# Putting the main loop of a delta-rule attention and feed-forward kernel into program order, with the block inversion spread over three steps

## The chip, the cores and the metric

The kernel runs on one core of one Trainium2 chip. The metric is the device time of one execution in microseconds (us), the median of several executions. Every kernel was run beside the kernel before on the same chip; not every experiment was on one and the same chip, so ratios compare better across experiments than medians do.

Short names: PE is TensorE's matmul part and PEld its weight load, DVE is VectorE, ACT is ScalarE, POOL is GpSimd. L571 is line 571 of that kernel's file; line numbers differ between the kernels.

## The reference

```python
# attention: batch 4, 8 heads, 768 positions, 48 dims
for t in range(S):
    y[:, :, t] = einsum('bhd,bhde->bhe', q[:, :, t], state)
    v_old = einsum('bhde,bhd->bhe', state, k_n[:, :, t])        # k_n = k / (|k| + 1e-6)
    state = state + beta * einsum('bhd,bhe->bhde', k_n[:, :, t], v[:, :, t] - v_old)
# feed-forward on x = y as (3072 tokens, 384)
h = x @ w_in                                                    # 384 -> 2048
out = (maximum(h, 0) + alpha * minimum(h, 0)) @ w_out           # 2048 -> 384
```

All is float32. The kernel does the recurrence in chunks of 64 positions: 24 steps (12 chunks times two pairs of batches). In each step a 64x64 triangular system is solved for each head. Its inverse is put together from two 32x32 inverses, and those of four steps are eliminated together on VectorE ("the inversion"), so that one inversion serves four steps.

## The kernel before

The parts that matter, with cuts marked by `# ...`. A `weave` is a loop that takes from several generators in proportion, so that their instructions are written in a mixed order. Up to `opening.close()` the written order is kept; after it, the tool's scheduler orders the instructions of each engine anew.

```python
EARLY = 6                                    # key Grams and key flips run this many steps ahead

def flips(n_k, n_q):                         # transposes of keys and queries on PE
    # ...
    flip(early(n_k), p_k)
    nc.scalar.copy(k_t[n_k]..., p_k)         # key copy ahead of the query flip, same PSUM tile
    flip(q_pad[n_q % NQ], p_q)
    nc.scalar.copy(q_t[n_q]..., p_q)

def eliminate(m):                            # the inversion, on DVE
    r = block[m]
    nc.vector.tensor_tensor(out=r, in0=r, in1=inside, op=ALU.mult)
    # ...
    for j in range(1, HB - 1):               # 30 pairs of product and update
        nc.vector.tensor_tensor(out=prod, ...)
        nc.vector.tensor_tensor(out=r[...], ...)
        yield
    nc.vector.transpose(turned[m]..., r)     # two whole turns of 128x1024
    nc.vector.transpose(inverse[m]..., r...)
    yield

def ffn_in(c):                               # 48 matmuls, 8 groups of 6; a p_ffn tile each, bufs=2
    # ... six matmuls into p_h, then:
    nc.scalar.activation(low, p_h, ACT.Relu, scale=-1.0)
    for i in range(2):
        nc.vector.scalar_tensor_tensor(out=g[:, i], in0=low[:, i], ..., in1=p_h[:, i])

def attention(n):
    place(n + 1)                 # ACT writes diag (4 instructions), inv (2), wgt (2)
    through_state(n)             # PE; DVE r; ACT y
    yield
    solve(n)                     # PE; DVE u
    yield
    outputs(n)                   # PE, and the state's update; DVE y, state
    between_1(n + 1)             # PE; ACT mid
    grams(n + EARLY, n + 1)      # PE; DVE kk and masks; ACT and DVE gather the blocks
    yield
    between_2(n + 1); to_ffn(n); flips(n + EARLY + 1, n + 2); prep(n + EARLY + 1)
    # ... loads
    scale_v(n + 1)
    yield

opening.close()
for n in range(NJ, N):           # NJ = 4, N = 24
    gens = [(attention(n), 4)]
    if (n + 2) % NJ == 0 and n + 2 < N:
        gens.append((eliminate((n + 2) // NJ), HB))         # the whole inversion in one step
    # ... and half a chunk of the feed-forward: 40 of its 80 matmuls
    weave(*gens)
```

## Time and profile before

| | before |
|---|---|
| median of its first runs | 768.65 us |
| span of the profiled run | 767.8 us |
| opening, 0 to 181.5 us | PE busy 155.9 |
| steps 4 and 5, 181.5 to 214.5 | PE busy 31.9 |
| steps 6 to 23, 214.5 to 722.25 (507.75 us) | PE busy 492.6, DVE 241.5, ACT 143.7 |
| the last chunk, 722.25 to the end | PE busy 41.4 of 45.6 |

The busy times are from the windows of the trace. PE is nearly full, so only what leaves PE idle, or slows its clock, can be won. In the long loop that is 507.75 - 492.6 = 15 us of idleness, besides the time lost to a halved clock, which counts as busy.

### The profile page before, as it was taken

The page shows a single profiled execution, that of the slowest core. Times are in us where ns is not written, and L with a number is a line of the kernel's source. Part 1 is how long each engine was busy: PE and PEld are TensorE (multiplying, and loading weights), DVE is VectorE, ACT ScalarE, POOL GpSimd, SP SyncE. Part 2 cuts the span into 40 slices and gives each one's busy share as a digit, 9 for nine tenths or more (in the row PEclk, how much of TensorE's full clock was granted, in tenths as well). Part 3 has the DMA queues.
Part 4 walks back from the last instruction along what each step waited for, and adds up shares of the span by engine and source line. Part 5 has one row for each costly group of instructions (what it writes and reads, how often), then busy time and mean ns, then how long its engine had stood idle before and what let it go on. Part 6 is the DMA issues. An engine that isn't in the chain of part 4 may idle for free.

```text
span 767.8 us, 20517 instructions
## 1 busy us (share of the span) xinstructions
PE 721.8 (94%) x8987; PEld 517.9 (67%) x8987; DVE 412.2 (54%) x979; ACT 251.7 (33%) x563; POOL 21.5 (3%) x80
## 2 busy tenths in 40 slices
PE   5999888898998999998999998999999999999997
PEld 4546666555676678666678667678667677687774
DVE  5886788896599224596224596214596233132020
ACT  3416656514424234125134124123114223021110
POOL 5000000010000000000000000000000000000000
PEclk9999899999999999999999999999999999999999
DMA  6815564311321122121122121111111110100000
GB/s 120 215 39 144 136 175 99 81 25 32 64 47 31 30 43 43 23 42 34 31 43 44 22 43 22 33 32 32 22 33 33 22 35 10 22 12 2 21 0 21
DMA packets 110185, 37.61 MB, mean 49 GB/s; under 512 B 103392, under 2 KB 106480, under 8 KB 110096
## 3 DMA queue, kind: packets, MB, share of 16 engines
q1 hardware_dynamic: 110064, 36.29, 21.7%
q8 instruction: 71, 1.16, 0.6%
q14 instruction: 18, 0.15, 0.1%
q10 hardware_dynamic: 32, 0.01, 0.0%
HBM read 31.56 MB, written 4.72 MB: 47 GB/s over the span
## 4 chain that ended last, share of the span: by engine, by line
PE 57%; DVE 29%; ACT 6%; issue 6%; POOL 1%; DMA 1%; SPq 0%; POOLq 0%; DVEq 0%; ACTq 0%
PE p_ffn L601 24%; PE p_ffn L571 21%; DVE prod L413 7%; DVE block L419 7%; DVE g L582 2%; PE p_big L503 2%; PE p_big L353 2%; PE p_big L530 2%; PE p_big L517 1%; DVE block L399 1%; DVE turned L424 1%; ACT diag L439 1%; DVE inverse L426 1%; DVE kk L359 1%; PE p_big L536 1%
## 5 line engine op out<-in xcount | busy, mean ns | idle before, releaser
L571 PE MATMUL p_ffn<-xt,w_in 128*128 128x256 f32 x1152 | 275.1, 391 | 14.1 <-DVE g L582 6.9
L601 PE MATMUL p_ffn<-w_out,g 128*128 128x384 f32 x768 | 262.2, 494 | 3.8 <-ACT diag L439 2.9
L571 PEld LDWEIGHTS p_ffn<-xt,w_in 128*128 128x128 f32 x1152 | 215.6, 193 | 50.0 <-ACT space_out L202 5.5
L601 PEld LDWEIGHTS p_ffn<-w_out,g 128*128 128x128 f32 x768 | 143.5, 192 | 95.9 <-ACT diag L439 3.2
L582 DVE SCALAR_TENSOR_TENSOR g<-low,al_t,p_ffn 128x256 f32<-128x256 f32 x192 | 83.6, 477 | 127.2 <-ACT low L579 127.1
L579 ACT ACTIVATE low<-p_ffn 128x512 f32<-128x512 f32 x96 | 56.8, 593 | 96.5 <-PE p_ffn L571 88.5
L413 DVE TENSOR_TENSOR prod<-block 128x30 f32<-128x30 f32 (+9 forms) x180 | 59.3, 330 | 5.5
L419 DVE TENSOR_TENSOR block<-block,prod 128x30 f32<-128x30 f32 (+9 forms) x180 | 59.4, 330 | 5.1
L544 DVE TENSOR_TENSOR y<-y,p_big 128x384 f32<-128x384 f32 x22 | 12.1, 552 | 58.8 <-PE p_big L530 58.8
L607 ACT COPY o_sb<-p_ffn 128x384 f32<-128x384 f32 x24 | 11.5, 478 | 90.1 <-PE p_ffn L601 90.1
L663 PE MATMUL p_ffn<-k_t,ident 128*128 128x512 f32 x76 | 37.9, 647 | 0.0
L439 ACT ACTIVATE diag<-inverse,which 64x128 f32<-64x128 f32 (+1 forms) x72 | 28.7, 399 | 23.1 <-PE p_big L476 17.5
L467 ACT COPY mid<-p_big 128x256 f32<-128x256 f32 x24 | 8.8, 372 | 80.1 <-PE p_big L463 80.1
L506 DVE TENSOR_TENSOR r<-v_raw,p_big 128x384 f32<-128x384 f32 x22 | 12.0, 550 | 37.0 <-PE p_big L503 36.8
L481 DVE TENSOR_TENSOR inv<-inv,p_big 128x256 f32<-128x256 f32 x24 | 10.0, 417 | 37.2 <-PE p_big L476 36.5
L439 ACT ACTIVATE inv<-inverse,which 128x256 f32<-128x256 f32 x48 | 21.7, 500 | 24.7 <-PE p_big L517 24.5
L663 PEld LDWEIGHTS p_ffn<-k_t,ident 128*128 128x128 f32 x76 | 14.8, 204 | 16.2 <-issue 15.7
L439 ACT ACTIVATE diag<-turned,which 128x256 f32<-128x256 f32 x24 | 11.6, 506 | 39.5 <-DVE turned L424 39.4
L353 PE MATMUL p_big<-k_t 48*64 48x64 f32 x768 | 18.3, 239 | 6.2 <-ACT k_t L337 4.3
L476 PEld LDWEIGHTS p_big<-diag,mid 64*64 64x64 f32 x768 | 14.3, 141 | 13.7 <-issue 9.8
L306 DVE TENSOR_REDUCE norm<-ksq 128x8 f32<-128x384 f32 x24 | 13.1, 546 | 17.1 <-ACT ksq L304 17.1
L392 ACT ACTIVATE same<-kk,which 128x256 f32<-128x256 f32 x24 | 12.2, 508 | 29.5 <-DVE kk L359 29.4
(94 smaller groups left out, 634.6 us busy)
## 6 DMA issues: line engine op xcount, KB each, us to landing
w_out<-in_moe_w_in_dram SPq DMA_DIRECT2D x12, 512.0 KB, 5.5
qp<-in_q_dram SPq DMA_DIRECT2D x48, 96.0 KB, 2.9
v_raw<-in_v_dram SPq DMA_DIRECT2D x48, 96.0 KB, 2.8
kl<-in_k_dram SPq DMA_DIRECT2D x96, 48.0 KB, 2.7
out_dram<-o_sb SPq DMA_DIRECT2D x48, 96.0 KB, 2.2
ke<-in_k_dram SPq DMA_DIRECT2D x46, 96.0 KB, 3.0
space_out<-in_moe_w_out_dram SPq DMA_DIRECT2D x11, 384.0 KB, 3.7
w_out<-in_moe_w_out_dram SPq DMA_DIRECT2D x5, 384.0 KB, 3.7
```

Of the source, the lines that this page charges most:

```text
L353: nc.tensor.matmul(p[half(t ^ a if w else t), a, w, g], k_t[n][dims(a), g, half(t)], rhs[n][dims(a), g, half(t)],)
L413: nc.vector.tensor_tensor(out=prod, in0=r[:, 0:j, j : j + 1].to_broadcast([128, j, n]), in1=r[:, j : j + 1, j + 1 : HB].to_broadcast([128, ...
L419: nc.vector.tensor_tensor(out=r[:, 0:j, j + 1 : HB], in0=r[:, 0:j, j + 1 : HB], in1=prod, op=ALU.add)
L439: nc.scalar.mul(dst[n % NE][to or rows, a.start * G : a.stop * G, cols], src[m][rows, heads], which[rows, i : i + 1],)
L476: nc.tensor.matmul(p[half(t), a, g], mid[n % 2][half(t ^ a), a * G + g], diag[n % NE][half(t ^ a), a * G + g, HB:C],)
L503: nc.tensor.matmul(p[half(t), a, w, g], x[n][dims(a), g, half(t)], state[bp][dims(a), t, g])
L530: nc.tensor.matmul(p[half(t), a, g], a_t[n][half(t ^ a), a * G + g], us[n][half(t ^ a), a, g])
L571: nc.tensor.matmul(p_h[:, i], w_in[:, t, (f + i) * 128 : (f + i + 1) * 128], xt[:, t], start=(t == 0), stop=(t == KT - 1),)
L579: nc.scalar.activation(low, p_h, ACT.Relu, scale=-1.0)
L582: nc.vector.scalar_tensor_tensor(out=g[:, i], in0=low[:, i], scalar=al_t[:, f + i : f + i + 1], in1=p_h[:, i], op0=ALU.mult, op1=ALU.add,)
L601: nc.tensor.matmul(p_o[bp], gs[f // 2][:, f % 2, bp * 128 : (bp + 1) * 128], w_out[:, f], start=(f == 0), stop=(f == FT - 1),)
L663: nc.tensor.matmul(p, ident, k_t[NJ - 1].rearrange("p g i -> p (g i)"))
```

## The change

Its intent: keep the program's order everywhere, give each step four pieces that each leave a quarter of a step between a producer and its user, take the inversion over three steps rather than one, and so keep PE full. The key Grams run 8 steps ahead, which the longer inversion needs.

```diff
-EARLY = 6
+EARLY = 8
+FIRST = 6
-    opening.enter_context(tc.manual_schedule(engines={      # ended by opening.close() before the loop
+    ctx.enter_context(tc.manual_schedule(engines={          # never ended

     def flips(n_k, n_q):
-            nc.scalar.copy(k_t[n_k].rearrange("p g i -> p (g i)"), p_k)
+            copies.append((k_t[n_k], p_k))
         # ...
+        for dst, src in copies:
+            nc.scalar.copy(dst.rearrange("p g i -> p (g i)"), src)

+    PIECES = 4
+    def turns(dst, src):                                    # a block turn in four quarters
+        n = HB // PIECES
+        for i in range(PIECES):
+            nc.vector.transpose(dst(slice(n * i, n * i + n)), src(slice(n * i, n * i + n)))
+            yield

     def attention(n):
-        place(n + 1)
+        place(n + 1, (0,))
         through_state(n)
+        between_1(n + 1)
+        place(n + 1, (1, 2))
         yield
         solve(n)
+        grams(n + EARLY, N)
+        between_2(n + 1)
+        scale_v(n + 1)
         yield
         outputs(n)
-        between_1(n + 1)
-        grams(n + EARLY, n + 1)
-        yield
-        between_2(n + 1)
+        next_state(n)
+        grams(N, n + 1)
+        load_late(n + 2)
+        squares(n + EARLY + 1)                              # apart from their roots (weigh)
+        yield
+        flips(n + EARLY + 1, n + 2)
         to_ffn(n)
-        flips(n + EARLY + 1, n + 2)
-        prep(n + EARLY + 1)
+        weigh(n + EARLY + 1)
         # ...

     for n in range(NJ, N):
-        if (n + 2) % NJ == 0 and n + 2 < N:
-            gens.append((eliminate((n + 2) // NJ), HB))
+        if n % NJ == 0 and n < N - NJ:
+            m = n // NJ + 1
+            blocks, left = eliminate(m), WHOLE + (PIECES if m > 2 else 0)
+            share = -(-left // 3)
+        if n % NJ < 3 and n < N - NJ:
+            gens.append((part(blocks, share), share))
```

Cut here: the Gram's left half is written straight into the gathered block and the right half into a tile of its own; the first five steps need three ACT writes fewer each; twelve units of the second inversion move forward in the opening (`SOON = 12`); the Grams of steps 10 and 11 are caught up before the loop, beside a quarter of a feed-forward output.

More of the change, by code (lines that the diff above doesn't have):

```diff
@@ L138, in load_late @@
                     nc.sync.dma_start(out=dst[a][half(t ^ a), :, 0:D], in_=src[a])
-    opening = ExitStack()
-    opening.enter_context(tc.manual_schedule(engines={
+    ctx.enter_context(tc.manual_schedule(engines={
         mybir.EngineType.PE, mybir.EngineType.DVE, mybir.EngineType.Activation,
@@ L290 @@
         nc.gpsimd.memset(t, 0.0)
-    stats, k_t, q_t, kk, a_t = {}, {}, {}, {}, {}
+    right = [const.tile([128, H + 1, HB], FP32, name=f"right{i}") for i in range(EARLY)]
+    for t in right:
+        nc.gpsimd.memset(t[:, 0], 0.0)
+    stats, k_t, q_t, a_t = {}, {}, {}, {}
     def by_parity(x):
@@ L301, in prep, with squares @@
             return
-        c, bp = steps[n]
+        squares(n)
+        weigh(n)
+    def squares(n):
+        if n >= N:
+            return
         ksq = work.tile([128, H, D], FP32, name="ksq", bufs=1)
@@ L306, in prep, with weigh @@
         nc.vector.tensor_reduce(out=norm, in_=ksq, axis=AXX, op=ALU.add)
+        stats[n] = norm
+    def weigh(n):
+        if n >= N:
+            return
+        c, bp = steps[n]
+        norm = stats[n]
         nc.scalar.sqrt(norm, norm)
@@ L332, in flips @@
         p = ps_big() if both else None
+        copies = []
         if n_k < N:
@@ L341, in flips @@
             q_t[n_q] = work.tile([128, G, 128], FP32, name="q_t")
-            nc.scalar.copy(q_t[n_q].rearrange("p g i -> p (g i)"), p_q)
+            copies.append((q_t[n_q], p_q))
+        for dst, src in copies:
+            nc.scalar.copy(dst.rearrange("p g i -> p (g i)"), src)
     def quarters():
@@ L357, in grams @@
         if n_k < N:
-            kk[n_k] = work.tile([128, H, C], FP32, name="kk", bufs=EARLY)
-            nc.vector.tensor_tensor(
-                out=kk[n_k].rearrange("p (a g) i -> p a g i", a=2),
-                in0=p[:, :, 0],
-                in1=stats[n_k][1][:, 0:2, :, None].to_broadcast([128, 2, G, C]),
-                op=ALU.mult,
-            )
+            w = stats[n_k][1][:, 0:2, :, None].to_broadcast([128, 2, G, HB])
+            for dst, cols in (
+                (gather(n_k), slice(0, HB)), (right[n_k % EARLY][:, 1:], slice(HB, C))
+            ):
+                nc.vector.tensor_tensor(
+                    out=dst.rearrange("p (a g) i -> p a g i", a=2), in0=p[:, :, 0, :, cols],
+                    in1=w, op=ALU.mult,
+                )
             keep(n_k)
@@ L385, with gather @@
     same, block, inverse, turned = {}, {}, {}, {}
-    def keep(n):
+    def gather(n):
         m, j = n // NJ, n % NJ
@@ L391, in keep, with turn_in @@
             same[m] = work.tile([128, NJ, H, HB], FP32, name="same", bufs=1)
-        nc.scalar.mul(same[m][:, j], kk[n][:, :, 0:HB], which[:, 0:1])
-        nc.vector.scalar_tensor_tensor(
-            out=same[m][:, j], in0=kk[n][:, :, HB:C], scalar=which[:, 1:2], in1=same[m][:, j],
-            op0=ALU.mult, op1=ALU.add,
-        )
-        if j == NJ - 1:
-            block[m] = work.tile([128, HB, HB], FP32, name="block", bufs=1)
-            nc.vector.transpose(
-                block[m].rearrange("b r c -> b c r"), same[m].rearrange("r j h c -> r c (j h)")
-            )
+        return same[m][:, j]
+    def keep(n):
+        m, j = n // NJ, n % NJ
+        for t in range(2):
+            own = slice(64 * t + HB, 64 * t + C)
+            if n < NJ:
+                nc.vector.tensor_copy(out=same[m][own, j], in_=right[n % EARLY][own, 1:])
+            else:
+                nc.scalar.copy(same[m][own, j], right[n % EARLY][own, 1:])
+        if j == NJ - 1 and m <= 2:
+            for _ in turn_in(m):
+                pass
+    PIECES = 4
[4 more added lines that the diff above has]
+            yield
+    def turn_in(m):
+        block[m] = work.tile([128, HB, HB], FP32, name="block", bufs=1)
+        yield from turns(
+            lambda x: block[m][:, :, x].rearrange("b r c -> b c r"),
+            lambda x: same[m][:, :, :, x].rearrange("r j h c -> r c (j h)"),
+        )
     def eliminate(m):
+        if m > 2:
+            yield from turn_in(m)
         r = block[m]
@@ L423, in eliminate, with changes @@
         turned[m] = work.tile([128, NJ * H, HB], FP32, name="turned", bufs=1)
-        nc.vector.transpose(turned[m].rearrange("c b r -> c r b"), r)
+        yield from turns(
+            lambda x: turned[m][:, :, x].rearrange("c b r -> c r b"), lambda x: r[:, x]
+        )
         inverse[m] = work.tile([128, NJ * H, HB], FP32, name="inverse", bufs=1)
-        nc.vector.transpose(inverse[m].rearrange("r b c -> r c b"), r.rearrange("b r c -> b c r"))
-        yield
+        yield from turns(
+            lambda x: inverse[m][:, :, x].rearrange("r b c -> r c b"),
+            lambda x: r[:, :, x].rearrange("b r c -> b c r"),
+        )
+    WHOLE = HB - 1 + 2 * PIECES
+    def changes(n):
+        return n > NJ
     def place(n, parts=(0, 1, 2)):
@@ L446, in place @@
         if 1 in parts:
-            put(diag, second, inverse, 1, a=slice(0, 1))
-            for t in range(2):
-                put(diag, second, inverse, 1, half(t), half(1 - t), slice(1, 2))
+            put(diag, second, inverse, 1, a=slice(0, 1 if changes(n) else 2))
+            if changes(n):
+                for t in range(2):
+                    put(diag, second, inverse, 1, half(t), half(1 - t), slice(1, 2))
         if 2 in parts:
             put(inv, first, inverse, 0)
-            put(inv, second, inverse, 1)
+            if changes(n):
+                put(inv, second, inverse, 1)
             w = stats[n][1]
@@ L463, in between_1 @@
             nc.tensor.matmul(
-                p[half(t ^ a), a, g], kk[n][half(t), a * G + g],
+                p[half(t ^ a if changes(n) else t), a, g],
+                right[n % EARLY][half(t), a * G + g : a * G + g + 2].rearrange("p b i -> p (b i)"),
                 diag[n % NE][half(t), a * G + g, 0:HB],
@@ L475, in between_2 @@
         for g, a, t in quarters():
+            x = half(t ^ a if changes(n) else t)
             nc.tensor.matmul(
-                p[half(t), a, g], mid[n % 2][half(t ^ a), a * G + g],
-                diag[n % NE][half(t ^ a), a * G + g, HB:C],
-            )
-        to = inv[n % NE].rearrange("p (a g) i -> p a g i", a=2)[:, :, :, HB:C]
-        nc.vector.tensor_tensor(out=to, in0=to, in1=p, op=ALU.add)
+                p[half(t), a, g], mid[n % 2][x, a * G + g], diag[n % NE][x, a * G + g, HB:C]
+            )
+        to, own = (
+            x[n % NE].rearrange("p (a g) i -> p a g i", a=2)[:, :, :, HB:C] for x in (inv, diag)
+        )
+        nc.vector.tensor_tensor(out=to, in0=to if changes(n) else own, in1=p, op=ALU.add)
     nv, rhs_, ys, us, xts = {}, {}, {}, {}, {}
@@ L532, in outputs @@
             )
-        if c < NCH - 1:
-            p_s = ps_big()[:, :, 0 : G * D].rearrange("p t (g d) -> p t g d", g=G)
-            for g, a, t in quarters():
-                nc.tensor.matmul(
-                    p_s[half(a), t, g], k_late[n % NKL][half(t ^ a), 2 * g + a],
-                    us[n][half(t ^ a), a, g],
-                )
         if c == 0:
@@ L546, in outputs, with next_state @@
             )
+    def next_state(n):
+        c, bp = steps[n]
         if c < NCH - 1:
-            nc.vector.tensor_tensor(out=state[bp], in0=state[bp], in1=p_s, op=ALU.subtract)
+            p = ps_big()[:, :, 0 : G * D].rearrange("p t (g d) -> p t g d", g=G)
+            for g, a, t in quarters():
+                nc.tensor.matmul(
+                    p[half(a), t, g], k_late[n % NKL][half(t ^ a), 2 * g + a],
+                    us[n][half(t ^ a), a, g],
+                )
+            nc.vector.tensor_tensor(out=state[bp], in0=state[bp], in1=p, op=ALU.subtract)
     def to_ffn(n):
@@ L632, in weave @@
                 live.pop(0)
+    SHARES = 4
     def attention(n):
-        place(n + 1)
+        place(n + 1, (0,))
         through_state(n)
+        between_1(n + 1)
+        place(n + 1, (1, 2))
         yield
         solve(n)
+        grams(n + EARLY, N)
+        between_2(n + 1)
+        scale_v(n + 1)
         yield
         outputs(n)
-        between_1(n + 1)
-        grams(n + EARLY, n + 1)
+        next_state(n)
+        grams(N, n + 1)
+        load_late(n + 2)
+        squares(n + EARLY + 1)
         yield
-        between_2(n + 1)
+        flips(n + EARLY + 1, n + 2)
         to_ffn(n)
-        flips(n + EARLY + 1, n + 2)
-        prep(n + EARLY + 1)
+        weigh(n + EARLY + 1)
         load_early(n + EARLY + 1 + NKE)
@@ L651, in attention @@
         load_v(n + 3)
-        load_late(n + 2)
-        scale_v(n + 1)
         yield
@@ L676, in pair @@
             outputs(i)
+            next_state(i)
             load_late(i + 2)
@@ L792, with prelude, catch_up @@
     fetch_out(len(stages))
+    blocks, SOON = eliminate(1), 12
     weave(
         (conv_out, PARTS_OUT - 10), (ffn_in(1), IN_PARTS),
-        (statics(2 * NJ, EARLY + 3), 2 * (EARLY + 4 - 2 * NJ) + 1),
+        (statics(2 * NJ, FIRST + 3), 2 * (FIRST + 4 - 2 * NJ) + 1), (part(blocks, SOON), SOON),
     )
-    flips(EARLY + NJ, NJ)
+    flips(FIRST + NJ, NJ)
     flips(N, NJ + 1)
-    prep(EARLY + NJ)
-    load_early(EARLY + NJ + NKE)
+    prep(FIRST + NJ)
+    load_early(FIRST + NJ + NKE)
     load_q(NJ + 2)
-    weave((eliminate(1), HB), (ffn_out(0, True), OUT_PARTS))
-    place(NJ)
-    between_1(NJ)
-    between_2(NJ)
-    grams(N, NJ)
-    scale_v(NJ)
-    opening.close()
+    weave((part(blocks, WHOLE - SOON), WHOLE - SOON), (ffn_out(0, True), OUT_PARTS))
+    def prelude(n):
+        place(n)
+        yield
+        between_1(n)
+        yield
+        between_2(n)
+        yield
+        grams(N, n)
+        scale_v(n)
+        yield
+    def catch_up():
+        for n in range(FIRST + NJ, EARLY + NJ):
+            grams(n, N)
+            flips(n + 1, N)
+            squares(n + 1)
+            yield
+            weigh(n + 1)
+            load_early(n + 1 + NKE)
+            yield
+    late = ffn_out(1)
+    few = OUT_PARTS // 4
+    weave((prelude(NJ), 4), (catch_up(), 2 * (EARLY - FIRST)), (part(late, few), few))
     def feed_forward():
@@ L815 @@
     tail = feed_forward()
-    late = ffn_out(1)
     for n in range(NJ, N):
-        gens = [(attention(n), 4)]
-        if (n + 2) % NJ == 0 and n + 2 < N:
-            gens.append((eliminate((n + 2) // NJ), HB))
+        gens = [(attention(n), SHARES)]
+        if n % NJ == 0 and n < N - NJ:
[4 more added lines that the diff above has]
+            gens.append((part(blocks, share), share))
         if n < NJ + 2:
-            gens.append((part(late, OUT_PARTS // 2), OUT_PARTS // 2))
+            gens.append((part(late, (OUT_PARTS - few) // 2), (OUT_PARTS - few) // 2))
         else:
```

## The prediction

> **What bounds the kernel now.** I read the page first: the busy shares, the slices and the chain that ended last.
>
> ```profile
> PE 721.8 (94%) x8987; PEld 517.9 (67%) x8987; DVE 412.2 (54%) x979; ACT 251.7 (33%) x563; POOL 21.5 (3%) x80
> ...
> PE   5999888898998999998999998999999999999997
> ...
> DVE  5886788896599224596224596214596233132020
> ...
> PE 57%; DVE 29%; ACT 6%; issue 6%; POOL 1%; DMA 1%; SPq 0%; POOLq 0%; DVEq 0%; ACTq 0%
> ```
>
> TensorE is busy 94% of the span, so all its idle time is 46 us. VectorE (DVE) peaks every sixth slice, and where it does PE falls below 9: these are the inversions, one for each four of the 24 attention steps. One inversion costs DVE about 27 us: 19.8 of products and updates (rows L413 and L419, 118.7 us over 6), three whole turns of about 2.0 (L399, L424, L426) and 1.2 for L406. In the loop it shares one step of about 26 us with another 6 us of attention and up to 6.4 us of PReLU work. It does not fit.
>
> What this costs I took from the chain in order of time, where L503 marks the start of a step:
>
> ```profile
> 300.99 1.08 PE p_big L503 x64
> 361.36 1.08 PE p_big L503 x64
> 416.52 1.08 PE p_big L503 x64
> 477.61 1.08 PE p_big L503 x64
> 589.83 1.08 PE p_big L503 x64
> 642.83 1.08 PE p_big L503 x64
> ```
>
> Two steps without an inversion take 416.52 - 361.36 = 55.2 us with PE full; those with one take 60.4 (from 300.99) and 61.1 (from 416.52). Two without key Grams and key flips take 53.0 (from 589.83). The timeline shows where the extra time goes in step 14:
>
> ```profile
> 455.37 2.83 PE L571 MATMUL p_ffn<-xt,w_in 128*128 128x256 f32 x12 [0.76 <-ACT low L579]
> ...
> 470.80 1.96 PE L571 MATMUL p_ffn<-xt,w_in 128*128 128x256 f32 x4 [1.35 <-DVE g L582]
> 472.78 1.11 PE L323 MATMUL p_big<-ident,qp 128*128 128x128 f32 x4
> ```
>
> The last idle 1.35 us came when ACT placed the finished inverses in one burst ahead of the PReLU's first half (low). PE has two p_ffn buffers; when both wait for low and g, it stops. Then its clock fell: the windows of 1 us show 0.50 from 471 to 474.
>
> **What the Trainium skill says.** "TensorE: Matmul & The Clock Gate", Part 1, What's actually happening: the clock halves after an idle window of about 3.4 us. Here 1.35 us of idleness in step 14 sufficed, while 1.36 us in step 10 did not, so the phase matters. The same page, Architectural detail, says that ScalarE and VectorE are strict FIFO. The manual opening agrees: at 55.52 ACT runs three diag writes (1.25 us), two inv (0.91), two wgt (0.40), just in the program's order. "PSUM — Partial Sum Buffer", Terms: two engines on one bank at once is an error, reads included. The trace agrees: the copy of y starts at 363.09, 0.04 us after r (362.50 plus 0.55), though both read finished matmuls. I rely on these for what order does to ACT.
>
> **The change part by part, counted as removed (-) and added (+) time.**
>
> *Inversion over three steps.* Loss of the four inversions in the loop: steps 6 and 7 took 276.65 - 214.47 = 62.2, so 7.0 over 55.2; then 5.2, 5.9, and 3.0 for steps 17 and 18 (57.1 against 54.1, the mean of 55.2 and 53.0). Sum 21.1. Spread, an inversion adds at most about 12 us to a step of 24 to 31 us that has 6 us of attention and at most 6.4 of g: DVE fits. Quarter turns are estimated from the fixed part of a DVE operation: 128x30 takes 178 ns and 128x240 takes 409, so 1.1 ns an element and about 0.15 fixed; a quarter is then at most 0.65 us and an inversion about 1.3 us longer, unimportant once spread, and g waits 0.6 rather than 2 us behind one. I leave 3 us for contention: -18.
>
> *Gram catch-up.* EARLY 8 moves the key Grams and flips of steps 16 and 17 before the loop: -2.2 in the loop (55.2 - 53.0).
>
> *Four pieces, fewer switches.* Between FFN runs and small matmuls about 0.2 us is lost at each switch (22 FFN-in instructions took 4.95 us, while the dense tail has 96 in 20.72, or 4.75 for 22). Before has five groups a step, since the query flips wait for the key copy; after has four, with both flips ahead of the copies. With that wait about 0.3 us a step, 18 steps: -5.4.
>
> *New burst on ACT.* Piece 1 now puts, in strict order, place part 0, y, mid, three diag writes, two inv, two wgt, ahead of the next low. Odd step, from its first matmul: r ends at 1.77 us (362.50 - 361.29 + 0.55), y at 2.30, mid at 2.70 (0.37 plus gap), then 1.25 + 0.91 + 0.40 and gaps to about 5.3; low to 5.95, two g (0.87) to 6.85, release about 6.95. PE needs 1.07 + 0.46 (between_1) = 1.53, then two FFN-in matmuls that finish one p_ffn group, six that finish the other (8 x 0.432 = 3.45), so at 5.1 it wants the first buffer for FFN-out. It waits about 1.85 us. Step boundaries fall at part 40 of 80, so every odd step has this, from 7 to 21: 8 x 1.85 = +15. In even steps the first group begins after piece 1 and is wanted at 7.0: no wait. There place 0 comes behind the output copy (0.48), so between_1 starts about 0.35 late: 8 x 0.35 = +3.
>
> *Clock.* A 1.85 us stop will often throttle. Idle times of 1.74, 2.13, 2.31 and 2.85 us in this trace were each followed by half-speed matmuls; 0.92 and 1.42 were not. At three in four, and 1.7 us lost each time (3.4 us at half), 8 x 0.75 x 1.7 = +10.
>
> *Opening.* ACT sheds three writes for each of steps 0 to 4 (two diag of 0.40, one inv of 0.50, less 0.1: about 1.15 us each), on the path near 55 to 60 and 80 to 88 us: about -4. The first Grams give up an ACT round trip (0.57 us idle each), but turn in quarters: 0. Twelve units (some 7 us of DVE) of the second inversion enter the stage from 119 to 150 us, where DVE is already near 85% busy: +4. The stage from 150 to 214 us becomes about 21 us of FFN-out, 10 of catch-up and 33 for steps 4 and 5 with their share of the third inversion: 64, as before. Sum 0, give or take 6.
>
> If the burst acts as computed: -18 - 2.2 - 5.4 + 15 + 3 + 10 + 0 = +2.4, or 771; I take 770 us. If it does not (some slack that I overlooked in ACT's order): -18 - 2.2 - 5.4 + 3 + 0 = -22.6, about 746.
>
> **The rivals.** (1) The gain arrives whole and PE is near 100% from 215 us on, 746 us. For it: non-inversion steps are full before, and all producers stand a quarter of a step ahead of their users; the many tuned constants of the change look measured. Against: the ACT arithmetic, from durations in this very trace. (2) The burst replaces the inversion's stall, 765 to 775. For it: step 14, where just such a burst stopped PE for 1.35 us. (3) DVE still stalls PE in the first third of an inversion: step 8 would carry 5.8 of attention, 5.8 of g and about 10 of turns and small products in 24.5 us, 88% with in-order waits; two us more for each of four, 8 us on top of (1), 754. Against: the long products fall in the FFN-out phase. (4) The opening, in which stalls already drop the clock to 0.83 to 0.91, decides: either way by 6 us.
>
> **Range and chances.** I give the burst 60%: 0.6 x 770 + 0.4 x 746 = 760. Each outcome has about 5 us of its own spread, so a tenth lies below 742 and a tenth above 775. Over 2% faster means under 753.3: nearly all of the other case, almost nothing of the burst's, 0.38. Slower means over 784, which would need the burst, all clock drops and a worse opening: 0.04.
>
> **What would show it.** Right if in the loop no step has DVE full and each starts 27 to 28 us after the one before on average. The burst is shown by FFN-out's first matmul of each odd step waiting about 1.85 us for g, with ACT busy without gap from y to wgt just before; it is refuted if PE runs through there. The clock is shown by windows at 0.50 just after. Switches: four small groups a step, no idle time before the query flips. Opening: step 6 should start near 214 us. The prediction is wrong if the loop from step 6 takes under 480 us or over 515 (now 507.8, from 214.47 to 722.25), or if the opening moves by over 6 us.

## The result, and the profile after

The changed kernel took 759.93 us in the median (4 runs, 759.29 to 761.07); the kernel before took 769.57 beside it (4 runs). The ratio is 0.987, with a 95% interval of 0.984 to 0.990. Ratios here are the mean time of one kernel's fast runs over that of the other's of the same rounds, so not quite the ratio of the medians. The change is faster by 1.3%, which is under the 2% that counts as a difference, and the point forecast was 760.0.

The page of the changed kernel (busy shares; PE and DVE in 40 slices of the span; the chain that ended last, by engine):

```profile
PE 715.1 (94%) x8987; PEld 521.4 (69%) x8987; DVE 406.1 (54%) x1041; ACT 245.2 (32%) x564; POOL 23.7 (3%) x88
...
PE   5979988889999999999999999999999999999997
...
DVE  6984788886987328736337746236744132032020
...
PE 73%; DVE 16%; ACT 8%; issue 2%; POOL 1%; POOLq 0%; DVEq 0%; ACTq 0%
```

DVE no longer stands at 9 in every sixth slice: the inversions are spread, and PE is at 9 from the tenth slice on. PE still idles 42 us, though. The chain of the changed kernel, in order of time, with the marks of step starts (L561 is through_state here), steps 10, 12, 14, 16, 18 and 20:

```profile
332.23 1.08 PE p_big L561 x64
388.08 1.12 PE p_big L561 x64
444.38 1.08 PE p_big L561 x64
499.78 1.08 PE p_big L561 x64
554.13 1.08 PE p_big L561 x64
608.30 1.08 PE p_big L561 x64
```

Two steps now take 55.9, 56.3, 55.4, 54.4 and 54.2 us. The 60 to 61 us of the steps with an inversion are gone, but two steps without key Grams, which took 53.0 before, take 54.2. Something new costs about 1.2 us in every two steps. The timeline of step 11 shows it (start, length, engine, line, tiles, count; in brackets the idle time just before and who ended it):

```profile
357.49 3.72 PE L631 MATMUL p_ffn<-xt,w_in 128*128 128x256 f32 x16
357.76 0.48 ACT L569 COPY y<-p_big 128x384 f32<-128x384 f32 x1 [2.38 <-DVE r L564]
358.14 0.38 ACT L523 COPY mid<-p_big 128x256 f32<-128x256 f32 x1
358.40 1.24 ACT L492 ACTIVATE diag<-inverse,which 128x128 f32<-128x128 f32 x3
359.65 0.91 ACT L492 ACTIVATE inv<-inverse,which 128x256 f32<-128x256 f32 x2
360.57 0.40 ACT L510 COPY wgt<-wgt 64x4 f32<-64x4 f32 x2
360.87 1.07 ACT L639 ACTIVATE low<-p_ffn 128x512 f32<-128x512 f32 x2
361.49 1.65 DVE L642 SCALAR_TENSOR_TENSOR g<-low,al_t,p_ffn 128x256 f32<-128x256 f32 x4 [3.76 <-ACT low L639]
362.51 2.17 PE L661 MATMUL p_ffn<-w_out,g 128*128 128x384 f32 x6 [1.30 <-DVE g L642]
```

ACT works without a gap from y at 357.76 to the end of wgt, and the PReLU's first half (low, L639) for a p_ffn group that PE had long finished comes only at 360.87. PE does its 16 dense instructions, finds both p_ffn buffers taken, and stops for 1.30 us until g frees one. This stop comes in each of the odd steps 7 to 21, eight times 1.30 us, always before FFN-out (L661). The windows of 4 us over the loop show no granted clock below 0.99: the stops do not throttle the clock here.

The windows of the two loops, from step 6 to the end of step 23 (stretch, length, then busy us and counts of PE, PEld, DVE, ACT and POOL, granted clock, DMA share, GB/s), first the kernel before:

```profile
214.50:722.25 507.75, 492.60 (x6436) 361.93 (x6436) 241.48 (x581) 143.68 (x314) 3.96 (x18) 0.99 0.15 30
```

and the changed kernel:

```profile
218.60:711.90 493.30, 481.17 (x6363) 359.52 (x6364) 224.41 (x579) 144.59 (x342) 4.56 (x20) 1.00 0.16 31
```

The loop is 14.45 us shorter. The first part, up to step 6, is 4.1 us longer (218.6 against 214.5), and the last chunk is the same. That makes the 10.3 us by which the span shrank. The idle time of PE in the changed loop is 12.1 us: eight stops of 1.30 (10.4), and waits on the inversion's work of 1.21 in step 6 and 0.21 in steps 8 and 12 (1.6).

The 4.1 us lost in the opening are seen in the windows from 52 us (same columns), in the kernel before:

```profile
52.00:60.00 8.00, 6.10 (x128) 3.53 (x120) 4.76 (x11) 4.91 (x14) 0.00 (x0) 0.79 0.43 134
60.00:68.00 8.00, 7.92 (x203) 4.54 (x200) 5.86 (x11) 1.87 (x6) 0.00 (x0) 1.00 0.46 142
```

and in the changed kernel:

```profile
52.00:60.00 8.00, 6.04 (x67) 4.44 (x68) 3.19 (x9) 2.85 (x9) 0.00 (x0) 0.50 0.44 133
60.00:68.00 8.00, 8.00 (x70) 3.89 (x69) 4.52 (x9) 0.00 (x0) 0.00 (x0) 0.50 0.22 65
```

The filler matmuls that keep PE's clock up during the first inversion ended at 48.9 us in this run (51.8 before). PE then waited 3.80 us for VectorE's masks, and its clock stayed at half until 69 us.

Both kernels issue the same 62 fillers. In the changed kernel's trace they came up to full speed sooner (10 of them ran from 24 to 28 us, against 6), and so they were done sooner. In the ten traces with 62 fillers they end anywhere from 48.9 to 51.8 us. So it is not shown that this loss belongs to the change: it varies from trace to trace, though the four timed runs of the changed kernel, at mean clocks of 0.981 to 0.983, look alike.

### The profile page after: what moved, and what is told of

It reads as the page before. It is cut to its first block, busy times and chain, and to the rows that moved or that the text cites. A ratio compares the mean times of both kernels' runs of the same rounds, so it can differ in the third digit from the quotient of the medians.

```text
span 757.5 us, 20590 instructions
## 1 busy us (share of the span) xinstructions
PE 715.1 (94%) x8987; PEld 521.4 (69%) x8987; DVE 406.1 (54%) x1041; ACT 245.2 (32%) x564; POOL 23.7 (3%) x88
## 4 chain that ended last, share of the span: by engine, by line
PE 73%; DVE 16%; ACT 8%; issue 2%; POOL 1%; POOLq 0%; DVEq 0%; ACTq 0%
PE p_ffn L661 34%; PE p_ffn L631 23%; PE p_big L561 3%; DVE g L642 3%; PE p_big L372 2%; PE p_big L588 2%; PE p_big L339 2%; DVE prod L456 2%; PE p_big L575 2%; PE p_big L533 2%; DVE block L462 2%; PE p_ffn L730 1%; PE p_big L604 1%; ACT diag L492 1%; ACT inv L492 1%
## 5 line engine op out<-in xcount | busy, mean ns | idle before, releaser
L631 PE MATMUL p_ffn<-xt,w_in 128*128 128x256 f32 x1152 | 270.4, 388 | 8.6 <-DVE g L642 5.6
L661 PE MATMUL p_ffn<-w_out,g 128*128 128x384 f32 x768 | 259.4, 490 | 12.8 <-DVE g L642 12.8
L661 PEld LDWEIGHTS p_ffn<-w_out,g 128*128 128x128 f32 x768 | 141.9, 190 | 106.1 <-ACT low L639 13.4
L639 ACT ACTIVATE low<-p_ffn 128x512 f32<-128x512 f32 x96 | 56.2, 593 | 114.3 <-PE p_ffn L631 85.8
L456 DVE TENSOR_TENSOR prod<-block 128x30 f32<-128x30 f32 (+9 forms) x180 | 58.9, 327 | 4.0
L422 ACT COPY same<-right 32x256 f32<-32x256 f32 x40 | 16.1, 402 | 59.4 <-DVE right L381 59.2
L595 DVE TENSOR_TENSOR y<-y,p_big 128x384 f32<-128x384 f32 x22 | 12.1, 548 | 40.3 <-PE p_big L588 40.3
L492 ACT ACTIVATE diag<-inverse,which 64x128 f32<-64x128 f32 (+2 forms) x62 | 25.5, 412 | 0.8
L324 DVE TENSOR_SCALAR norm<-norm 128x8 f32<-128x8 f32 x24 | 6.5, 271 | 30.9 <-ACT norm L323 30.9
L518 PE MATMUL p_big<-diag,right 64*64 64x32 f32 x768 | 18.6, 223 | 4.1 <-DVE a_t L390 3.8
L579 DVE TENSOR_TENSOR u<-p_big,wgt 128x384 f32<-128x384 f32 x24 | 13.2, 552 | 16.8 <-PE p_big L575 16.7
L569 ACT COPY y<-p_big 128x384 f32<-128x384 f32 x22 | 10.5, 479 | 34.4 <-DVE r L564 34.4
L372 PEld LDWEIGHTS p_big<-k_t 48*64 48x64 f32 x768 | 15.9, 155 | 8.2 <-ACT k_t L361 5.4
L361 ACT COPY k_t<-p_big 128x512 f32<-128x512 f32 x24 | 13.9, 578 | 23.1 <-PE p_big L339 23.0
```

What stands on the lines that cost most here:

```text
L372: nc.tensor.matmul(p[half(t ^ a if w else t), a, w, g], k_t[n][dims(a), g, half(t)], rhs[n][dims(a), g, half(t)],)
L422: nc.scalar.copy(same[m][own, j], right[n % EARLY][own, 1:])
L456: nc.vector.tensor_tensor(out=prod, in0=r[:, 0:j, j : j + 1].to_broadcast([128, j, n]), in1=r[:, j : j + 1, j + 1 : HB].to_broadcast([128, ...
L492: nc.scalar.mul(dst[n % NE][to or rows, a.start * G : a.stop * G, cols], src[m][rows, heads], which[rows, i : i + 1],)
L518: nc.tensor.matmul(p[half(t ^ a if changes(n) else t), a, g], right[n % EARLY][half(t), a * G + g : a * G + g + 2].rearrange("p b i -> p ( ...
L631: nc.tensor.matmul(p_h[:, i], w_in[:, t, (f + i) * 128 : (f + i + 1) * 128], xt[:, t], start=(t == 0), stop=(t == KT - 1),)
```

## The experiments

All start from the changed kernel, and all gave correct results. The kernel before took 768.5 to 771.3 us in the median beside them. One variant deadlocked and never ran: with the whole inversion in the first of the three steps, its new inverses would have had to overwrite those that later steps still read.

### Late inv writes

```diff
         between_1(n + 1)
-        place(n + 1, (1, 2))
+        place(n + 1, (1,))
         yield
+        place(n + 1, (2,))
         solve(n)
```

> The changed kernel with one move: the two inv writes and the two wgt copies on ScalarE go from the end of piece 1 to the start of piece 2. Theory (the burst on ScalarE in piece 1 holds the PReLU's low back, and PE stops for want of a p_ffn buffer): the burst is 1.31 us shorter (0.91 + 0.40), the stop of 1.30 us in the odd steps 7 to 21 goes, 8 x 1.3 = 10.4 us, so about 749.5 us, with no wait of FFN-out's first matmul on g over 0.3 us. Rival (the stop is made by VectorE, which is late with r or g, or the moved writes only move the stop to piece 2): 758 to 760 us, and the stop stays or turns up behind piece 2.

Measured: 748.4 us (6 runs, 741.75 to 749.05), ratio to the kernel before 0.972 (0.969 to 0.975). The timeline of the same step 11:

```profile
352.38 3.72 PE L631 MATMUL p_ffn<-xt,w_in 128*128 128x256 f32 x16
...
353.29 1.24 ACT L492 ACTIVATE diag<-inverse,which 128x128 f32<-128x128 f32 x3
354.44 0.57 ACT L639 ACTIVATE low<-p_ffn 128x512 f32<-128x512 f32 x1
355.04 0.87 DVE L642 SCALAR_TENSOR_TENSOR g<-low,al_t,p_ffn 128x256 f32<-128x256 f32 x2 [2.43 <-ACT low L639]
356.06 2.17 PE L661 MATMUL p_ffn<-w_out,g 128*128 128x384 f32 x6
...
356.82 0.91 ACT L492 ACTIVATE inv<-inverse,which 128x256 f32<-128x256 f32 x2
357.75 0.40 ACT L510 COPY wgt<-wgt 64x4 f32<-64x4 f32 x2
```

Low now follows the diag writes at once, the FFN-out line has no bracket, and the inv writes fall where ACT is idle. No stop over 0.4 us is left in the loop, which takes 481.3 us, 12.0 less. The 12.0 us are nearly all of PE's idle time in the changed loop (12.1): the waits of 1.21 and 0.21 us went as well. The burst on ACT is shown to be the cause of the stops, and the rival falls. By the way, the one run of six at 741.75 us had a mean clock of 0.993 where the others had 0.981 to 0.983.

### 35 fillers

```diff
-BUSY = 31
+BUSY = 35
```

> The changed kernel with 35 instead of 31 filler matmuls during the first inversion. In the changed kernel the fillers end at 48.9 us, PE then waits 3.8 us for the masks and its clock is at half from 52 to 69 us; in the kernel before they ended at 51.7 us. Theory (the opening's loss is this cold clock): PE idles about 0.5 to 1.9 us there, the clock is low for 4 us at most as before, and the first FFN matmul comes 4 to 6 us earlier than now (76.5 us): 754 to 756 us. Rival (the opening is bound by the conversions of the weights on VectorE, so an earlier pair of steps only waits later; and step 6 is late because of the twelve units of inversion moved forward): within 1 us of 760.

Measured: 754.22 us (5 runs), ratio 0.981 (0.979 to 0.983). The windows of this kernel (same columns):

```profile
52.00:60.00 8.00, 8.00 (x117) 4.69 (x115) 4.12 (x11) 3.23 (x10) 0.00 (x0) 1.00 0.43 133
60.00:68.00 8.00, 8.00 (x212) 4.76 (x210) 6.22 (x12) 0.48 (x1) 0.00 (x0) 1.00 0.45 133
```

The clock is full throughout, and PE issues 212 instructions from 60 to 68 us instead of 70. Step 7 starts 5.3 us earlier (238.63 against 243.89). The cold clock is what the opening lost; the rival falls.

### The inversion in one step, all else as changed

```diff
-            share = -(-left // 3)
-        if n % NJ < 3 and n < N - NJ:
-            gens.append((part(blocks, share), share))
+            if m > 2:
+                gens.append((part(blocks, PIECES), 4 * PIECES))
+        if n % NJ == 2 and n < N - NJ:
+            gens.append((part(blocks, WHOLE), WHOLE))
```

> The changed kernel, but the inversion after its turn-in runs whole in one step of four (6, 10, 14, 18), as it did before the change; all else as changed. Theory (spreading it over three steps is what removed the loss of 21.1 us that the kernel before had in those steps): 20 us come back, more if strict order costs more: 778 to 785 us, with PE idle in those steps and clock drops. Rival (the loss before came from the scheduler's order, and program order alone cures it): under 765 us.

Measured: 808.77 us (4 runs), ratio 1.051. That is 49 us more than the changed kernel, over twice what I expected, and 40 us more than the kernel before. The loop takes 546.5 us instead of 493.3. PE's stops in step 10 and the next (timeline):

```profile
352.08 1.10 PE L631 MATMUL p_ffn<-xt,w_in 128*128 128x256 f32 x4 [2.23 <-ACT ksq L313]
357.97 2.83 PE L631 MATMUL p_ffn<-xt,w_in 128*128 128x256 f32 x12 [1.30 <-DVE g L642]
365.64 7.27 PE L631 MATMUL p_ffn<-xt,w_in 128*128 128x256 f32 x20 [3.38 <-DVE g L642]
381.26 3.87 PE L661 MATMUL p_ffn<-w_out,g 128*128 128x384 f32 x6 [3.14 <-DVE g L642]
```

What PE waits for comes after the inversion's work written ahead of it on DVE. Before the third stop, for instance, low was ready at 361.5 us, and g began only at 364.6, after six products and updates and some other work. In the last stop DVE waited too: r had stood behind the final turns, so the burst on ACT began late. The last two stops were each followed by matmuls at about half speed (20 in 7.27 us, where 4.48 is usual). So spreading is essential in strict order. It does not give the worth of spreading by itself, since the kernel before had the inversion in one step as well and lost only 21 us: its order of DVE's work was the scheduler's, not the program's.

### The scheduler orders the loop

```diff
-    ctx.enter_context(tc.manual_schedule(engines={
+    opening = ExitStack()
+    opening.enter_context(tc.manual_schedule(engines={
     # ...
+    opening.close()
     def feed_forward():
```

> The changed kernel with the manual order ended after the opening, as in the kernel before: the tool's scheduler orders the loop. Theory (program order's only cost is the burst; the scheduler spread the ScalarE writes in the kernel before): the stops of 1.30 us in odd steps go, but the key and query flips may part again (0.3 us a step): 748 to 758 us. Rival (program order is itself what gains, the scheduler makes worse waits with these pieces): over 762 us.

Measured: 771.28 us (6 runs, 767.53 to 773.07), ratio 1.005. The stops of 1.30 us before FFN-out are gone, as expected, but the gain is gone too. Where the inversion's products (L457) run, in the windows for those instructions alone (stretch, length, DVE busy, clock, DMA share, GB/s):

```profile
270.00:280.00 10.00, 4.22 (x11) 1.00 0.39 73
280.00:290.00 10.00, 3.83 (x13) 1.00 0.09 21
```

and in the changed kernel (L456):

```profile
290.00:300.00 10.00, 1.90 (x7) 1.00 0.39 71
300.00:310.00 10.00, 1.91 (x5) 1.00 0.07 13
310.00:320.00 10.00, 2.01 (x5) 1.00 0.04 7
320.00:330.00 10.00, 2.08 (x6) 1.00 0.42 81
```

The program spreads the inversion over three steps in both, but the scheduler pulls it together into some 20 us again. PE waits for g just after (1.64 and 1.83 us, at 293 and 298 us), and for 3.76 us in step 6, where no product of the inversion ran near. The rival holds: spreading survived only in program order, and program order bore the inversion only when it was spread.

How much the pulling together costs is not shown, for the scheduler did more. The profiled span is 8.2 us longer than the changed kernel's. Of that, 4.2 us lie in the loop from step 6 (497.5 us, with 13.8 us of idleness on PE instead of 12.1, and three throttled stretches), and 6.7 in steps 4 and 5 (35.5 us instead of 28.7); the part before was 2.7 us shorter.

### A longer burst

```diff
-            put(inv, first, inverse, 0)
+            for _ in range(3 if n > FIRST + 1 else 1):
+                put(inv, first, inverse, 0)
```

> The changed kernel with the first inv write of each later step done three times (same values), so ScalarE's burst is 2 x 0.455 = 0.91 us longer. It asks after the clock, which I predicted would fall at three of four stops and which fell at none of the eight. If the stop is what the burst sets: 8 stops of 2.2 us instead of 1.3, +7.3 us, about 767. Theory A (a stop of 1.3 us is short enough for the clock, one of 2.2 is not: the share of idle time in a window decides): half-speed windows follow in most odd steps, another 1.5 us each, 775 to 780 us. Theory B (the steady rest of the loop protects the clock whatever the stop): no half-speed windows, 767 us. Even steps may also begin to wait, up to 0.9 us each, 7 us more, to be read from the trace.

Measured: 775.14 us (4 runs, 772.82 to 777.27), ratio 1.008. The stops before FFN-out are 2.39 or 2.40 us in all eight odd steps, 1.09 more than before. The first of them:

```profile
251.05 2.17 PE L662 MATMUL p_ffn<-w_out,g 128*128 128x384 f32 x6 [2.39 <-DVE g L643]
```

In five even steps (8 to 16) a stop of 0.73 to 1.24 us appeared, as I had allowed. The profiled run (span 771.0 us, 13.5 more than the changed kernel's) has no window below 0.99 in the loop: eight times 1.09 makes 8.7 us, the even stops give 4.4, and the rest is less than one throttled stretch costs. So this run shows no half-speed windows, as theory B had it, although the median lies in theory A's range. The other timed runs were up to 4 us slower at a mean clock of 0.978 to 0.981 instead of 0.985; where theirs fell is not recorded. The next experiment shows why this run says little for B.

### A burst longer still

The same edit with seven writes instead of three.

> The changed kernel with the first inv write done seven times, so ScalarE's burst is 6 x 0.455 = 2.7 us longer than in the changed kernel and stops of about 4.1 us come in the odd steps, 2 to 3 us in the even ones. After stops of 2.4 us (three times) the clock did not fall in the loop. If the clock falls once a stop is longer than about 3.4 us (the window of the TensorE page): half-speed windows at each odd step from 7 to 21, 1.7 us each on top of the stops: 8 x 2.7 + 7 x 2.2 + 8 x 1.7 = 51, about 811 us. If it falls for another reason (many short stops near each other): no half-speed windows, about 797 us.

Measured: 822.69 us (4 runs), ratio 1.065, some 11 us above the first of the two forecasts. The stop is 4.54 us in each of the eight odd steps, and half-speed windows follow every one of them, for example (windows of 4 us, same columns as above):

```profile
252.00:256.00 4.00, 1.16 (x3) 0.82 (x4) 1.66 (x4) 2.24 (x6) 0.00 (x0) 0.93 0.00 0
256.00:260.00 4.00, 4.00 (x100) 2.33 (x98) 0.68 (x2) 0.00 (x0) 0.00 (x0) 0.64 0.01 4
```

The even steps' two stops of 1.0 to 1.4 and 0.5 to 2.2 us had none. In these loops, then, stops of 1.30 and 2.39 us never lowered the clock (16 of 16) and stops of 4.54 always did (8 of 8). But the length of a stop is not what decides: 2.37 us at 130 us did lower it in the changed kernel, and 1.35 us in step 14 of the kernel before.

The clock records of the traces settle more. In each trace the changes of the clock lie whole multiples of 3.41 us apart (in the changed kernel 109.89, 113.30, 130.37, 133.78, 147.44 and 150.85 us). If each trace is cut into stretches at that pace, the idle time within one stretch tells. Two stretches and the one after each (same columns), in the changed kernel:

```profile
126.96:130.37 3.41, 1.04 (x6) 0.62 (x5) 3.27 (x11) 3.25 (x7) 0.88 (x2) 1.00 0.00 0
130.37:133.78 3.41, 3.41 (x10) 2.70 (x9) 3.24 (x11) 0.00 (x0) 0.00 (x0) 0.50 0.63 159
```

and in the longer burst:

```profile
536.77:540.18 3.41, 1.45 (x7) 0.94 (x5) 0.58 (x2) 3.19 (x8) 0.00 (x0) 1.00 0.00 0
540.18:543.59 3.41, 2.97 (x66) 1.93 (x67) 3.27 (x10) 0.00 (x0) 0.00 (x0) 1.00 0.00 0
```

The first had 2.37 us of idleness and the clock fell; the second had 1.96 and it stayed. The 14 traces hold 950 full-speed stretches in which PE ran nothing but feed-forward matmuls. The clock fell after all 39 with 2.01 us of idleness or more, after one with 1.96, and after none of the other 910, whose highest is 2.00. So the 2.39 us stops were harmless by luck: all eight lay across a cut, with at most 1.96 us on one side of it. Stretches that also hold small matmuls fell with less (1.53 us in step 14 of the kernel before, 467.48 to 470.89); how much a small matmul counts stays open.

### Whole turns

```diff
-    PIECES = 4
+    PIECES = 1
```

> The changed kernel with whole turns of the block (one of 2 us) instead of quarters. Theory (the quarters matter little once the inversion is spread: PE idled only 1.6 us in the loop on VectorE): a turn of 2 us can hold g back up to 1.5 us more in steps 8, 12 and 16 (turn-in during FFN-in): +1 to +4 us, 761 to 764 us. Rival (the quarters are essential): a stop over 1 us at each of the 9 turns of the three last inversions and clock drops, over 768 us. Second rival (quarters cost more than they bring): under 759.

Measured: 754.16 us in the median, ratio 0.981, but in two groups: three runs at a mean clock of 0.993 took 749.86 to 751.54 us, and three at 0.982 to 0.984 took 756.79 to 757.48. The profiled run is of the first group, its fillers ended at 51.3 us and its opening was not cold. So the 6 us in the median are mostly the opening's chance. Set against the changed kernel, whose four runs all had 0.981 to 0.983, the second group is 2.8 us faster (757.2 against 759.9); the trace has 1.8 us of that in the loop, where the waits in steps 6, 8 and 12 vanish though one stop grows to 1.88 us. My theory missed, and the second rival holds here: the quarters cost a little and bring nothing. No trace of the second group was kept.

### None of the second inversion moved forward

```diff
-    blocks, SOON = eliminate(1), 12
+    blocks, SOON = eliminate(1), 0
```

(with the then empty generator dropped from the weave)

> The changed kernel with none of the second inversion's twelve units moved into the stage of FFN-in(1). Theory (the 7 us of VectorE work lengthen that stage, which VectorE bounds, as much as they shorten the next): the stage ends some 6 us earlier (159 to about 153 us), the inversion's stage is then bound by VectorE again and ends some 6 us later against its start: within 2 us of 760. Rival (the forward move is worth it, PE fills the inversion's stage with FFN-out): over 762.

Measured: 761.64 us (6 runs), ratio 0.991: 1.7 us more than the changed kernel, within the 2 us of the theory. The move is nearly an even exchange between two stages.

### The two cures together

Late inv writes and 35 fillers.

> Late inv writes (as e1) and 35 fillers (as e2) together. If both theories hold, the gains add, since one lies in the loop and the other in the opening: 744 to 747 us. If only the burst theory holds, 749 to 750; if only the cold clock, 755.

Measured: 740.5 us (4 runs, 740.08 to 741.88), ratio 0.963 (0.961 to 0.966). Of the 19.4 us against the changed kernel, the loop gives 11.9 (481.4 us) and the opening 7.2 (step 6 at 211.35). The gains add, and the sum is 3.5 us better than the lower end of what I expected: the opening gave 7.2 us here against 5.3 in the run with 35 fillers alone. This version beats both kernels.

### Key copy between the flips

```diff
-            copies.append((k_t[n_k], p_k))
+            nc.scalar.copy(k_t[n_k].rearrange("p g i -> p (g i)"), p_k)
```

> The changed kernel with the copy of the key flip put back between the key flips and the query flips. Theory (my term for the switches: PE's wait for that copy was about 0.3 us a step): the wait returns in the steps with both flips, 6 to 15, and a few earlier: PE idle of some 0.3 to 0.6 us before the query flips in each, +3 to +6 us: 763 to 766. Rival (the gain came only from having four groups of small matmuls instead of five, the copies' place is nothing): within 1 us of 760.

Measured: 767.17 us (6 runs), ratio 0.994 (0.991 to 0.997): 7.2 us more than the changed kernel, a little over the theory's range (by the ratios 5.5 us, within it). PE waits 0.78 us (even steps) or 0.68 us (odd) before the query flips in each of the steps 6 to 15; ten of them make 7.3, the loop is 500.6 instead of 493.3, and the steps without key flips are unchanged. The first of these waits in the loop:

```profile
238.37 0.66 PE L339 MATMUL p_big<-ident,qp 128*128 128x128 f32 x4 [0.78 <-ACT k_t L354]
```

The rival falls.

### Both cures and whole turns

> Late inv writes, 35 fillers and whole turns. The run with whole turns alone gained 6 us, of which its trace puts 6.4 us before step 6 (218.59 to 212.16, no long cold clock) and 1.8 us in the loop. If the first is only the timing of the fillers, which 35 of them give anyway, whole turns add 0 to 2 us to 740.5: 738 to 741. If whole turns help the opening by themselves: 734 to 736. If quarters matter once the burst is gone (g has less slack lost elsewhere): over 742.

Measured: 741.11 us (5 runs), ratio 0.961 (0.959 to 0.964), against 0.963 with quarters: no difference that the runs can tell. The first of the three expectations comes nearest, though 741.11 lies just above its range.

### Both cures and six units moved forward

`SOON = 6` instead of 12.

> Late inv writes, 35 fillers and six instead of twelve units of the second inversion moved forward. If the forward move is a fair exchange between two stages (as the run with none of it suggests, 761.6 against 759.9): within 1.5 us of 740.5. If twelve is too many for the stage that VectorE bounds: 736 to 738. If fewer leave PE idle in the inversion's stage: over 742.

Measured: 741.63 us (5 runs), ratio 0.962 (0.9595 to 0.9647): the same as with twelve.

## Why the prediction was right or wrong

The point, 760.0 us, agrees with the measured 759.93, but that is luck. It was the mean of two cases, 770 with the burst on ACT and 746 without. The burst came, so on the working's own terms its branch was 770, and it was 10 us too high. These are the terms for the 10.3 us that the span shrank, measured against predicted:

| term | predicted | measured | from |
|---|---|---|---|
| the inversion's loss in the loop, less contention | -18 | -19.5 | 21.1 lost before; PE waits 1.6 on it now |
| Grams and flips moved out of the loop | -2.2 | -2.2 | taken over, not measured apart |
| burst on ACT, odd steps | +15 | +10.4 | eight stops of 1.30 |
| place 0 behind the output copy, even steps | +3 | +1.2 | between_1 starts 1.05 to 1.17 us after the step in the nine even steps, 0.97 in the odd ones |
| clock after the stops | +10 | 0 | no window under 0.99 in the loop |
| switches and flips | -5.4 | -4.4 | what remains of the loop's -14.5, not measured apart |
| opening up to step 6 | 0 | +4.1 | 214.5 to 218.6 |

*The inversion.* The mechanism was right. (One reading was not exact: PE's slices below 9 stand partly one slice after DVE's 9, and the last inversion has none.) What the prediction missed is that it takes two parts of the change together: left to the scheduler, the spread inversion was pulled together and the gain was gone (771.28 us), and program order with the inversion in one step is far worse than the kernel before (808.77 us).

*The burst.* Right in place, order and number of stops, too large in size: 1.85 us predicted, 1.30 measured. From the step's first matmul, ACT's low began at 4.91 us, not 5.3, since the writes follow each other without the gaps that I had added; and PE wanted the buffer at 5.25, not 5.1. Moving two writes and two copies removed all eight stops, as the arithmetic said (10.4 us expected, 12.0 gained in the loop).

*The clock.* This is the step that failed: "At three in four, and 1.7 us lost each time (3.4 us at half), 8 x 0.75 x 1.7 = +10". It counted the lengths of idle times, and its list left out 1.63 us at 141.8 us, after which the clock stayed at full. Its 1.74 us lay in a stretch (102.25 to 105.67) with 1.1 us of small matmuls besides. Among feed-forward matmuls the clock fell only from about 2.0 us of idleness in one stretch of 3.41 us. By that measure neither the predicted 1.85 us nor the measured 1.30 us could lower it, wherever the stop lay.

*The opening.* "Sum 0, give or take 6" held at +4.1, but for another reason than any term of it: the fillers ended before PE had its next work, and the clock went cold. No term had considered where the fillers end. Since that end varies from trace to trace with the same 62 fillers (48.9 to 51.8 us), the 4.1 us are not shown to be an effect of the change. Four more fillers gained 5.7 us. The lighter ACT work that I counted as -4 is not visible by itself.

*Switches.* The size is about right, but it is only what remains of the sum, and its cause is not shown. The key copy's place is worth 7.3 us in strict order: a wait of about 0.73 us in the ten steps that have both flips. In the loop of the kernel before, PE waited for that copy only 1.3 us in all; in step 14 the scheduler had put four feed-forward matmuls into the wait. So little of the gain over the kernel before can come from there.

*Rivals.* Rival 1 (746 us) was nearly reached once the burst was moved (748.4). Rival 2 had the right mechanism, but its 765 to 775 us was too high, since the stops came to 10.4 us against the 19.5 that the inversion gave back. Rival 3 (DVE still stalls PE in the first third of an inversion, 8 us) was 1.6 us. Rival 4, the opening, moved by 4.1 us. The quarters, which the prediction called unimportant, were just that.

## What to carry to other kernels

Fixing the order of a loop by hand moves the bound to the bursts: look in each piece for the engine that gets the most instructions in a row, and ask which short instruction of another chain stands behind them; moving four instructions by a quarter of a step was worth more here than the whole change. Work that is spread in the source is only spread on the chip if the order is kept, so such parts are to be judged together. A filler that keeps the clock up has to last until the next work is really there. Whether a stop costs clock is read from the idle time in one stretch between the points at which the clock can change, 3.41 us apart here, and not from the length of the stop; one harmless run proves little when all its stops lie across such a point.

## What the Trainium skill lacked or had wrong

- "TensorE: Matmul & The Clock Gate", Part 1, What's actually happening, gives one idle window of about 3.4 us as what halves the clock, and calls the window free-running. The length and the free running agree with the traces: changes of the clock come whole multiples of 3.41 us apart, whatever the kernel does. But a window need not be idle throughout: 2.0 us of idleness in 3.41 sufficed among feed-forward matmuls (40 falls in 950 stretches, lowest 1.96 us; highest without a fall 2.00). The section does not say how much idleness it takes, nor how small matmuls count; the runs did not settle the second.
- The same section says that the ramp is run-variable and its penalty under 1% of a typical kernel's span. Here the same kernel took 749.9 to 751.5 us or 756.8 to 757.5, with mean clocks of 0.993 and 0.982 to 0.984: 6 us, 0.8%. That agrees in size (a second cold stretch, not the start), but it is enough to hide a small effect, so such runs have to be compared by their clock.
- "Perfetto Trace Analysis", Optimization Strategy, says that a gap that keeps recurring can mean too few buffers for the next tile. The gap of 1.30 us was such a one (both p_ffn buffers taken), but no buffer was added: another order on ACT freed the buffer in time.
- The same page, Optimizing Scalar/DVE Operations, says that breaking up instructions may let work complete sooner. Here turns of 2.0 us in four quarters of 0.60 to 0.64 us on average gained nothing (741.11 us whole, 740.5 in quarters). "VectorE: DVE Perf Modes", The three transpose paths, has no duration for float32: on average 128x1024 took 1.95 to 2.01 us, and 128x256 took 0.60 to 0.64.
- No page was found on what a scheduler does with work that the source spreads out; here it drew three steps' worth together into some 20 us, and the kernel whose loop it ordered took 11 us more (771.28 against 759.93), not all of it for that reason.
